# Two tiles' results in one bank, every second group's rows summed in three parts by VectorE, and the first taps ahead of the weights' loads, in a fused attention and feed-forward kernel

## The chip, the core and the metric

The kernel runs on one core of a Trainium2 chip. The metric is the time of one execution on the device, in microseconds (us). The engines of a core run at the same time and each takes its instructions in the order in which they stand: PE (TensorE) multiplies matrices, DVE (VectorE) and ACT (ScalarE) work element by element and reduce, POOL (GpSimd) works element by element on SBUF alone, and SP (SyncE) issues most of the transfers. An instruction that waits holds back all that stand behind it on its engine.

## What is computed

A local attention over windows of seven positions, and on its result a feed-forward block: a product with `w_in`, a SoLU (h times softmax of h), a layer norm and a product with `w_out`. Cut to what matters:

```python
w = softmax(weight_gen)                        # over the 7 taps, per position and head
out[s] = sum(w[s, k] * x_pad[s + k] for k in range(7))     # heads of 24 columns, 192 in all
x = out.reshape(33280, 192)
h = x @ w_in                                   # 192 -> 1024
solu = h * softmax(h)
ln = (solu - mean(solu)) / sqrt(var(solu) + 1e-6) * g_ln
return ln @ w_out                              # 1024 -> 192
```

There are 8 sequences of 4160 positions: 33280 rows, in 260 tiles of 128 rows.

## The kernel before

Each of the 128 partitions holds a run of 260 consecutive positions, so that a tile t is position t of every run. The work goes through five engines, tile by tile:

- **POOL** makes the attention for a group of four tiles at once (`attention`, called by `attend`; the first four tiles go in two groups of two). One product makes seven weighted rows `pr` (L174, 5376 elements a partition); an addition puts parts 3 to 5 on parts 0 to 2 (L180, 2304 elements); a second one makes two parts `half` of the four that are left (L182, 1536 elements). POOL also makes two of the seven steps of the taps' softmax (`softmax_taps`: the subtraction L114 and the scaling L126), once per chunk. A chunk is what is loaded at once: 4, then 8, then 8 tiles, then 16.
- **DVE** adds the two parts of `half` into the rows `a` (`last_sum`, L433, the step `fin`). `half` has two buffers, `a` has three.
- **PE** transposes `a` (step `xT`, two tiles at a time, L450), ACT and DVE split the result into a high and a low half, and PE multiplies with `w_in` in twelve matmuls (`first_product`, step `mm1`, L491 and L494) into a PSUM tile `h` of two banks, of which there are three.
- DVE finds the maximum (L505), ACT the exponentials (L509), DVE their product with h (L515), ACT the squares (L521) and the high half of the result (L528), DVE the low half (L532). `h` is free after these.
- SP transposes the result by a DMA (`transpose_s`, L540) into one of six buffers `hlT`; PE multiplies it with `w_out` in 24 matmuls (`second_product`, step `mm2`, L580) into `po`, one bank of PSUM with one buffer; ACT scales `po` into the output rows (`finish`, step `out`, L591), and SP stores four tiles at once.

At the start the weights, which come as pairs of 32-bit words, are converted by DVE and ACT (`float_of_double`, L241 to L260), and the first product waits for that. The squares of x (L145) and their sums (L151) feed a scale.

The order of all these steps on each engine is not written out: `issue_order` is a planner that holds a cost and the earlier steps for each step, and at each moment gives an engine the step with the lowest key among those that are ready. The key is the tile's number plus an offset per kind of step, from the table `URGENCY`. What comes out is the program's fixed order. The steps ahead of the planner (loads, constants, the first chunk's taps) stand in the order of the code.

Of the kernel before, what the change touches and what calls it, by code (L numbers as in the profile page):

```python
# [26 lines left out]
def tile_kernel(ctx: ExitStack, tc: tile.TileContext, x, weight_gen, w_in, w_out, g_ln, out):  # L27
    nc = tc.nc
# [24 lines left out]
    ps_a = ctx.enter_context(tc.tile_pool(name="ps_a", bufs=1, space=PSUM))  # L53
    ps_o = ctx.enter_context(tc.tile_pool(name="ps_o", bufs=1, space=PSUM))

    nc.scalar.preload_act_table_set("natural_log_exp_and_others")

    x_run = x.rearrange("b (q t) d -> (b q) t d", t=RUN)
# [112 lines left out]
    def attention(xt, wt, t, n, half):  # L171

        pr = att.tile([P, K, TG, D], F32, name="pr", bufs=1)[:, :, :n]
        nc.gpsimd.tensor_tensor(  # L174
            out=window(pr, 0, [(TG * D, K), (HG, n * H), (1, HG)]),
            in0=window(xt, t * D, [(D, K), (HG, n * H), (1, HG)]),
            in1=window(wt, t * HK, [(1, K), (K, n * H), (0, HG)]),
            op=ALU.mult,
        )
        nc.gpsimd.tensor_tensor(out=pr[:, :3], in0=pr[:, :3], in1=pr[:, 3:6], op=ALU.add)  # L180

        nc.gpsimd.tensor_tensor(  # L182
            out=half, in0=window(pr, 0, [(2 * TG * D, 2), (D, n), (1, D)]),
            in1=window(pr, TG * D, [(5 * TG * D, 2), (D, n), (1, D)]), op=ALU.add,
        )
# [2 lines left out]
    w_in = w_in.bitcast(I32)  # L188
    w_out = w_out.bitcast(I32)
    load_x(0)  # L190
    raw_a = att.tile([P, 2 * FF], I32, name="raw_a", bufs=1)

    raw_b = big.tile([P, FF], I32, name="hl", bufs=3)
# [29 lines left out]
    column = const.tile([P, 1], F32, name="column")  # L223
    minus = const.tile([P, P], F32R, name="minus")
    nc.vector.tensor_scalar_mul(minus, ident, -1.0)

    for step in range(TAP_STEPS):
        softmax_taps(0, step)

    scratch = {}  # L230

# [50 lines left out]
    def norm_of_first(step):  # L282
        if step < 3:
            nc.vector.tensor_reduce(
                sq[:, 4 + step : 5 + step], first["b" if step == 2 else step], axis=AX.X,
                op=ALU.max, apply_absolute_value=True,
            )
        elif step == 3:
            nc.scalar.activation(sq[:, 4:7], sq[:, 4:7], AF.Square)
        elif step == 4:  # L290
            first["total"] = ps_o.tile([P, 512], F32, name="po")
            nc.tensor.matmul(first["total"][:, :3], ones, sq[:, 4:7], start=True, stop=True)
        elif step == 5:
            nc.vector.tensor_reduce(
                first["total"][:, 8:9], first["total"][:, :3], axis=AX.X, op=ALU.add
            )
        elif step == 6:
            nc.scalar.activation(column, first["total"][:, 8:9], AF.Ln, scale=1.05 * FF)
            nc.scalar.activation(column, column, AF.Exp, scale=0.5)
# [27 lines left out]
    def scale_and_sum(f, step):  # L327
        if "w2" not in second:
            second["w2"] = att.tile([P, NJ, D], F32, name="raw_a", bufs=1)
        w2 = second["w2"]  # L330
        j0, j1 = JP * f, JP * (f + 1)
        if step == 0:
            for j in range(j0, j1):
                nc.scalar.activation(
                    w2[:, j, :], second[f][:, (j - j0) * D : (j - j0 + 1) * D], AF.Copy,
                    scale=g[:, j : j + 1],
                )
        elif step == 1:
            if f == 0:
                second["sums"] = ps_o.tile([P, 512], F32, name="po")  # L340
            for j in range(j0, j1):
                nc.tensor.matmul(
                    second["sums"][:, :D], ones, w2[:, j, :], start=j == 0, stop=j == NJ - 1
                )
        elif step == 2:
            junk = big.tile([P, FH], F32, name="frac")
            nc.scalar.activation(
                junk[:, : JP * D], w2[:, j0:j1].rearrange("p j d -> p (j d)"), AF.Square,
                accum_out=sq[:, f : f + 1],
            )  # L350
# [54 lines left out]

    def stat_group(t):

        n = 2 if t < 2 * TG else TG
        return n if t % n == n - 1 else 0


    def group(t):

        if t < TG:
            return 2 if t % 2 == 0 else 0
        return TG if t % TG == 0 else 0

    def attend(t):
        n = group(t)
        c = max(n for n in range(NCHUNK) if starts[n] <= t)  # L420
        half = att.tile([P, 2, TG, D], F32, name="half", bufs=2)[:, :, :n]
        half_of[t] = half
        attention(xs[c], ws[c], t - starts[c], n, half)

# [148 lines left out]
    def second_product(t):  # L573
        hlT = hlT_of.pop(t)

        free = t >= RUN - TG and t % 2 == 1
        po = ps_h.tile([P, FF], F32, name="h") if free else ps_o.tile([P, 512], F32, name="po")
        terms = [(half, j, w) for j in range(NJ) for half, w in ((0, 0), (0, 1), (1, 0))]
        for n, (half, j, w) in enumerate(terms):
            nc.tensor.matmul(  # L580
                po[:, :D], hlT[:, half * NJ + j, :], w2_hl[:, j, w, :],
                start=n == 0, stop=n == len(terms) - 1,
            )
        p_of[t] = po
# [58 lines left out]


URGENCY = dict(
    a00=3.1, a01=2.3, a02=-28.9, a03=-6.5, a04=-3.6, a10=80, a11=-25.4, a12=-13, a13=-10, a14=10.4,
    attA=85.1, attB=2.4, b0=120.9, b1=-144.6, b2=138.3, b3=-1.5, b4=54.3, c00=-28.1, c01=85.1,
    c02=6.8, c10=-25.3, c11=31.3, c12=-72.7, c20=99.4, c21=-5.6, c22=10.2, c30=-149.7, c31=-14.5,
    c32=-100.3, dup=52.6, exp=-129.5, f0=8.2, f1=-120.4, f2=-71.5, f3=-118.4, f4=-66.1, f5=-45.6,
    fin=18.4, hi=-11, lo=33, lw=18.7, lx0=10.2, lx1=-115.4, lx2=-109.1, lx3=-20.7, max=-30,  # L650
    mm1=25.5, mm2=0.4, n0=-7.5, n1=11.8, n2=-1.8, n3=-113.6, n4=-8.6, n5=-69, n6=-123.6, od=-6.9,
    out=-81.2, p30=22.9, p31=0.5, p4=9.7, p5=12.6, p6=11.6, p70=-10.2, p71=-8.7, p80=20.3, p81=5.9,
    q00=7.1, q01=-5.1, q02=118.9, q10=-15.7, q11=20.7, q12=16.8, q20=100.6, q21=-95.2, q22=20.4,
    q30=143.8, q31=81.5, q32=98.3, solu=-7.6, sq=5, t0=5.1, t1=-3.7, t2=77.9, t3=44.1, t4=-26.5,
    t5=110.1, t6=267.2, tr=-13, v00=170.9, v01=5.1, v02=44, v03=0.2, v1=54.2, v2=58.8, v3=-12.2,
    v4=1, v5=21.2, xT=-66.9, xhi=-46.7, xld=30,
)


def issue_order(run, starts, group, stat_group, loads):  # L660
# [5 lines left out]

    PE, DVE, ACT, SP, POOL = range(5)
    SAME, CROSS = (25, 127, 143, 0, 102), 130
    free = [3000, 5900, 5000, 12000, 9050]
    steps, number = [], {}  # L670

    def add(name, t, engine, cost, *after, ready=0):
# [7 lines left out]
    parts = ["a0", "b", "a1", *(f"c{f}" for f in range(4))]  # L680
    for n, part in enumerate(parts):
        w_in, size = n < 3, 512 if n < 3 else 384
        at = (9000, 10500, 12000)[n] if w_in else 15000
        before = () if w_in else (f"{parts[n - 3]}4", "n" + {"a0": "0", "a1": "1", "b": "2"}[parts[n - 3]]) if n < 6 else ("q00",)
        if n:
            before += (parts[n - 1] + "0",)
        once(part + "0", DVE, 3 * (60 + size), *before, ready=at)
        once(part + "1", ACT, 2 * (190 + 0.85 * size), part + "0")
        once(part + "2", DVE, 3 * (60 + 1.04 * size), part + "1")
        if w_in:  # L690
            once(part + "3", ACT, 190 + 0.75 * size, part + "2")
            once(part + "4", DVE, 60 + 1.04 * size, part + "3")
            once("n" + {"a0": "0", "a1": "1", "b": "2"}[part], DVE, 60 + 1.04 * size, part + "2")
        else:
            f = n - 3
            once(f"q{f}0", ACT, 700, part + "2")
            once(f"q{f}1", PE, 660, f"q{f}0", *([f"q{f - 1}1"] if f else ["n6"]))
            once(f"q{f}2", ACT, 520, f"q{f}0")
    add("p30", 0, DVE, 868, ("q31", 0), ("mm1", 1))
# [31 lines left out]
        add("v4", t, DVE, 80, ("v3", t))  # L731
        add("v5", t, ACT, 240, ("v4", t))

    add("v00", 0, ACT, 1800, ready=9000)
    add_norms(0, 0)
    for c in range(1, len(starts) - 1):
        t, before = starts[c], starts[c - 1] if c > 1 else -1
# [7 lines left out]
        for part in range(4 if whole else 1):  # L745
# [3 lines left out]
                load = min(part + 1, loads - 1) if whole else loads - 1  # L749
                add(f"v0{part}", t, ACT, size, (f"lx{load}", t))  # L750
            else:
                add(f"v0{part}", t, ACT, size, ready=15000)
        add_norms(c, t)
        n = (starts[c + 1] - t) * 8
        on = (DVE, POOL, ACT, DVE, ACT, DVE, POOL)
# [13 lines left out]
    for i, t in enumerate(groups):  # L769
# [3 lines left out]
            after.append(("t6", starts[c]))  # L773
        if c > 1:
            after.append((f"lx{loads - 1}", starts[c]))
        add("attA", t, POOL, 14990 if full else 7500, *after, ready=15000 if c == 1 else 9000)
        add("attB", t, POOL, 3510 if full else 1800, ("attA", t), ("fin", groups[i - 2] if i > 1 else -1))
        old = t // 4 * 4 - 12
        add("dup", t, ACT, 307 if full else 200, ("fin", t))
        add("fin", t, DVE, 1710 if full else 880, ("attB", t), ("xT", old + 2 if old >= 0 else -1))  # L780


    def on_vector(t):
# [15 lines left out]
    for t in range(run):  # L799
# [15 lines left out]
        if t >= run - 4:  # L815
            after += [("mm1", run - 1), ("out", t - 2)]
        else:
            after.append(("out", t - 1))
        add("mm2", t, PE, 2170, ("tr", t), *after)
        add("out", t, ACT, 304, ("mm2", t), ("f5", stats_of[t]), ("od", t // 4 * 4 - 5))  # L820
        if n := stat_group(t):
            tiles = range(t - n + 1, t + 1)
            add("f0", t, ACT, 190, ("v5", starts[chunk_of(t)]), *(("exp", u) for u in tiles))
# [101 lines left out]
```

## Time and profile before

| what | us |
|---|---|
| median of three runs | 1347.44 |
| lowest and highest run | 1345.54, 1348.4 |
| the profiled execution's own time | 1347.67 |
| its span, first to last instruction | 1345.8 |
| its mean granted TensorE clock | 0.994 |
| POOL's last instruction ends | 1290.43 |

A row of a time line has its start, its length, the engine, the line of the kernel, the operation, and the tile that it writes and those that it reads; in brackets stands how long the engine was idle before it, and what ended that. A row of a group of equal instructions has their count, their busy time in all and the mean in ns of one, then the idle time ahead of them. A row of windows has busy time (and count) for each engine in that stretch, then the granted clock, the DMA engines' share and GB/s. PEld is the loading of weights into TensorE, beside its matmuls.

### The profile page before, as it was taken

The numbers are of one execution on the slowest core, as the hardware profiler recorded it, in microseconds if no ns is written. First come the engines' busy times: TensorE is split into PE (matmuls) and PEld (weight loads), VectorE is DVE, ScalarE is ACT, GpSimd is POOL, SyncE is SP. The second block draws the span as 40 slices with busy tenths as digits, with TensorE's granted clock in tenths as the row PEclk, the third lists the DMA queues.
The fourth block names the chain that finished last, engine by engine and source line by source line (L and its number), as shares of the span: only waits on it lengthen the run. The fifth ranks groups of instructions, "written<-read, shape, count | busy, mean of one in ns | idle before, by whom it ended". The sixth has DMA issues, their size and how long they took to land.

```text
span 1345.8 us, 25810 instructions
## 1 busy us (share of the span) xinstructions
PE 1246.8 (93%) x9900; PEld 970.8 (72%) x9900; DVE 1210.2 (90%) x1588; ACT 1162.8 (86%) x2318; POOL 1247.7 (93%) x241
## 2 busy tenths in 40 slices
PE   0588899999999999999999999999999999999997
PEld 0365677777777777777777777777777777777776
DVE  5988899999999999999999999999999999889994
ACT  3778889889898988989898998989898898988886
POOL 5989899999999999999999999999999999999930
PEclk9899999999999999999999999999999999999999
DMA  5277668797886889688797968878787877976776
GB/s 180 74 159 169 139 134 201 123 207 137 155 179 134 196 137 208 125 179 163 129 202 140 191 140 180 162 128 203 140 193 137 183 150 138 183 134 123 133 134 130
DMA packets 565307, 210.31 MB, mean 156 GB/s; under 512 B 544456, under 2 KB 545864, under 8 KB 565184
## 3 DMA queue, kind: packets, MB, share of 16 engines
q1 hardware_dynamic: 563208, 206.55, 75.7%
q10 hardware_dynamic: 1976, 2.12, 0.6%
q8 instruction: 78, 1.28, 0.4%
q14 instruction: 45, 0.37, 0.1%
HBM read 46.15 MB, written 25.56 MB: 53 GB/s over the span
## 4 chain that ended last, share of the span: by engine, by line
ACT 43%; DVE 35%; issue 11%; PE 7%; DMA 2%; POOL 1%; SPq 0%; ACTq 0%; POOLq 0%
ACT hl L528 12%; ACT e L521 12%; DVE h L515 11%; DVE hl L532 11%; ACT e L509 9%; DVE stats L505 5%; DVE a L433 4%; ACT junk L145 3%; PE po L580 3%; PE h L494 2%; ACT x_hi L458 2%; ACT ot L591 2%; DMA hlT<-hl 2%; PE h L491 1%; DVE x_lo L479 1%
## 5 line engine op out<-in xcount | busy, mean ns | idle before, releaser
L174 POOL TENSOR_TENSOR pr<-xt,wt 128x5376 f32<-128x5376 f32 (+1 forms) x66 | 631.6, 9569 | 2.7
L580 PE MATMUL po<-w_hl,hlT 128*128 128x192 f16 x6192 | 555.1, 246 | 17.3 <-ACT ot L591 12.6
L580 PEld LDWEIGHTS <-hlT 128*128 128x128 f16 x6240 | 505.9, 98 | 83.2 <-issue 75.5
L515 DVE SCALAR_TENSOR_TENSOR h<-h,row,e 128x1024 f32<-128x1024 f32 x260 | 333.8, 1285 | 19.1 <-ACT e L509 16.9
L528 ACT ACTIVATE hl<-h 128x1024 f16<-128x1024 f32 x260 | 266.0, 1029 | 98.4 <-DVE h L515 55.4
L532 DVE SCALAR_TENSOR_TENSOR hl<-h,hl 128x1024 f16<-128x1024 f32 x260 | 316.5, 1218 | 36.8 <-ACT e L521 34.4
L180 POOL TENSOR_TENSOR pr<-pr 128x2304 f32<-128x2304 f32 (+1 forms) x66 | 333.0, 5045 | 5.2
L505 DVE TENSOR_REDUCE stats<-h 128x1 f32<-128x1024 f32 x260 | 316.3, 1217 | 3.9 <-PE h L494 3.3
L509 ACT ACTIVATE e<-h,stats 128x1024 f32<-128x1024 f32 x260 | 293.3, 1128 | 16.1 <-DVE stats L505 15.5
L521 ACT ACTIVATE e<-h,stats 128x1024 f32<-128x1024 f32 x260 | 293.0, 1127 | 1.1 <-DVE hl L532 1.0
L494 PE MATMUL h<-wa_hi,x_hi 128*128 128x512 f32 x520 | 234.0, 450 | 0.0
L182 POOL TENSOR_TENSOR half<-pr 128x1536 f32<-128x1536 f32 (+1 forms) x66 | 225.8, 3421 | 5.2
L494 PE MATMUL h<-wa_lo,x_hi 128*128 128x512 f32 x520 | 206.4, 397 | 0.0
L494 PE MATMUL h<-wa_hi,x_lo 128*128 128x512 f32 x520 | 205.9, 396 | 0.0
L494 PEld LDWEIGHTS h<-wa_hi,x_hi 128*128 128x128 f32 x520 | 98.1, 189 | 107.1 <-issue 95.5
L491 PE MATMUL h<-wb_hi,x_hi 64*128 64x512 f32 x520 | 131.0, 499 | 17.1 <-DVE hl L532 11.2
L433 DVE TENSOR_REDUCE a<-half 128x768 f32<-128x1536 f32 (+1 forms) x66 | 117.2, 1776 | 0.0
L591 ACT ACTIVATE ot<-po,stats 128x192 f32<-128x192 f32 x258 | 112.4, 436 | 3.6 <-PE po L580 3.6
L494 PEld LDWEIGHTS h<-wa_hi,x_lo 128*128 128x128 f32 x520 | 98.4, 189 | 23.2
L494 PEld LDWEIGHTS h<-wa_lo,x_hi 128*128 128x128 f32 x520 | 99.0, 190 | 12.0
L491 PE MATMUL h<-wb_hi,x_lo 64*128 64x512 f32 x520 | 104.2, 395 | 0.0
L450 PE MATMUL pa<-ident,a 128*128 128x128 f32 x520 | 81.2, 278 | 23.9 <-DVE x_lo L479 13.2
(89 smaller groups left out, 1072.0 us busy)
## 6 DMA issues: line engine op xcount, KB each, us to landing
out_dram<-ot SPq DMA_DIRECT2D x65, 384.0 KB, 3.3
xt<-in_x_dram SPq DMA_DIRECT2D x30, 576.0 KB, 4.8
xt<-in_x_dram SPq DMA_DIRECT2D x30, 480.0 KB, 4.4
wt<-in_weight_gen_dram SPq DMA_DIRECT2D x15, 448.0 KB, 4.8
hlT<-hl SPq DMA_TRANSPOSE x260, 4.7
xt<-in_x_dram SPq DMA_DIRECT2D x3, 384.0 KB, 4.6
raw_a<-in_moe_w_in_dram ACTq DMA_DIRECT2D x2, 512.0 KB, 7.4
raw<-in_moe_w_out_dram ACTq DMA_DIRECT2D x1, 768.0 KB, 12.2
```

The costliest lines, as they stand in the source:

```text
L174: nc.gpsimd.tensor_tensor(out=window(pr, 0, [(TG * D, K), (HG, n * H), (1, HG)]), in0=window(xt, t * D, [(D, K), (HG, n * H), (1, HG)]), i ...
L180: nc.gpsimd.tensor_tensor(out=pr[:, :3], in0=pr[:, :3], in1=pr[:, 3:6], op=ALU.add)
L182: nc.gpsimd.tensor_tensor(out=half, in0=window(pr, 0, [(2 * TG * D, 2), (D, n), (1, D)]), in1=window(pr, TG * D, [(5 * TG * D, 2), (D, n), ...
L491: nc.tensor.matmul(h[:, fs], lhs[rows, 1, :], rhs[rows], start=n == 0, stop=False)
L494: nc.tensor.matmul(h[:, fs], lhs[:, 0, :], rhs[:, fs], start=False, stop=n == 2)
L505: nc.vector.tensor_reduce(stat(t, NMAX), h_of[t], axis=AX.X, op=ALU.max, negate=True)
L509: nc.scalar.activation(e, h_of[t], AF.Exp, bias=stat(t, NMAX), accum_out=stat(t, Z))
L515: nc.vector.scalar_tensor_tensor(out=h, in0=h, scalar=row(t, SCALE), in1=e, op0=ALU.mult, op1=ALU.mult, accum_out=stat(t, M))
L521: nc.scalar.activation(e_of.pop(t), h_of[t], AF.Square, bias=stat(t, M), scale=-float(FF), accum_out=stat(t, Q),)
L528: nc.scalar.activation(hl[:, 0, :], h_of[t], AF.Copy, scale=2.0**14)
L532: nc.vector.scalar_tensor_tensor(out=hl[:, 1, :], in0=h_of[t], scalar=2.0**14, in1=hl[:, 0, :], op0=ALU.mult, op1=ALU.subtract,)
L580: nc.tensor.matmul(po[:, :D], hlT[:, half * NJ + j, :], w2_hl[:, j, w, :], start=n == 0, stop=n == len(terms) - 1,)
```

## The change

- One PSUM tile `results` of one bank is made at the start. A second product writes columns 0 to 191 of its first or second half, by the tile's number odd or even; in the planner a second product now follows the evacuation of the tile two before, not of the one before. The small sums of the preparation use the same bank.
- In every second group of four tiles (t // 4 odd, 32 of them) POOL leaves three parts: the addition over 2304 elements writes to `half` directly, and one over 768 elements puts the seventh part on the first. DVE's sum reads three parts there. `half` has room for three parts in both buffers.
- The last four tiles go in two groups of two, for the attention and for the statistics.
- The first chunk's taps are put ahead of the loads of the weights in the code.
- The planner has a new table `URGENCY` and new costs and ready times.

```diff
+    results = ps_o.tile([P, 512], F32, name="po")
...
+        if half.shape[1] == 3:
+            nc.gpsimd.tensor_tensor(out=half, in0=pr[:, :3], in1=pr[:, 3:6], op=ALU.add)
+            nc.gpsimd.tensor_tensor(out=half[:, 0], in0=half[:, 0], in1=pr[:, 6], op=ALU.add)
+            return
         nc.gpsimd.tensor_tensor(out=pr[:, :3], in0=pr[:, :3], in1=pr[:, 3:6], op=ALU.add)
...
     load_x(0)
+    for step in range(TAP_STEPS):
+        softmax_taps(0, step)
     raw_a = att.tile([P, 2 * FF], I32, name="raw_a", bufs=1)
...
-    for step in range(TAP_STEPS):
-        softmax_taps(0, step)
...
-            first["total"] = ps_o.tile([P, 512], F32, name="po")
+            first["total"] = results[:, 384:]
...
-                second["sums"] = ps_o.tile([P, 512], F32, name="po")
+                second["sums"] = results
...
-        n = 2 if t < 2 * TG else TG
+        n = 2 if t < 2 * TG or t >= RUN - TG else TG
...
-        if t < TG:
+        if t < TG or t >= RUN - TG:
...
+    def parts(t):
+
+        return 3 if t // TG % 2 else 2
...
-        half = att.tile([P, 2, TG, D], F32, name="half", bufs=2)[:, :, :n]
+        half = att.tile([P, 3, TG, D], F32, name="half", bufs=2)[:, : parts(t), :n]
...
-        po = ps_h.tile([P, FF], F32, name="h") if free else ps_o.tile([P, 512], F32, name="po")
+        po = ps_h.tile([P, FF], F32, name="h") if free else results[:, t % 2 * 256 :]
...
-    a00=3.1, a01=2.3, a02=-28.9, a03=-6.5, a04=-3.6, a10=80, a11=-25.4, a12=-13, a13=-10, a14=10.4,
+    a00=0.7, a01=13.5, a02=111.2, a03=-14.2, a04=63.6, a10=-30.7, a11=-18.7, a12=20.5, a13=-10.6,
...
-    free = [3000, 5900, 5000, 12000, 9050]
+    free = [3000, 5600, 7700, 12000, 6200]
...
-            after.append(("out", t - 1))
+            after.append(("out", t - 2))
...
-        add("out", t, ACT, 304, ("mm2", t), ("f5", stats_of[t]), ("od", t // 4 * 4 - 5))
+        add("out", t, ACT, 304, ("mm2", t), ("out", t - 1), ("f5", stats_of[t]), ("od", t // 4 * 4 - 5))
```

On POOL, in the first 60 us after its first full group, the order before is this, from the scaling of the third chunk's taps (`wt<-wt,wy`) on; `wt<-wt,wm` is the subtraction for a later chunk:

```order
L126 TENSOR_TENSOR wt<-wt,wy 128x448
L114 TENSOR_TENSOR wt<-wt,wm 128x896
L174 TENSOR_TENSOR pr<-xt,wt 128x5376
L180 TENSOR_TENSOR pr<-pr 128x2304
L182 TENSOR_TENSOR half<-pr 128x1536
L126 TENSOR_TENSOR wt<-wt,wy 128x896
L174 TENSOR_TENSOR pr<-xt,wt 128x5376
```

At the same place of the changed kernel:

```order
L128 TENSOR_TENSOR wt<-wt,wy 128x448
L176 TENSOR_TENSOR pr<-xt,wt 128x5376
L183 TENSOR_TENSOR half<-pr 128x2304
L184 TENSOR_TENSOR half<-half,pr 128x768
L116 TENSOR_TENSOR wt<-wt,wm 128x896
L176 TENSOR_TENSOR pr<-xt,wt 128x5376
```

The subtraction for the next chunk moved from ahead of the group's product to behind the group, and the group (tiles 12 to 15) ends in three parts.

On ACT, at the start of the program, the order before is this (`wt` are the taps, `raw_a`, `raw_101` and `g` the weights, `junk,squares_x` the squares of x):

```order
L79 DMA xt<-in_x_dram 15x1152 x4
L195 DMA raw_a<-in_moe_w_in_dram 128x1024 x2
L202 DMA raw_101<-in_moe_w_out_dram 128x4x384
L206 DMA g<-in_moe_g_ln_dram 128x8x1
L118 ACTIVATE wt<-wt 128x224
L145 ACTIVATE junk,squares_x<-xt 128x1920
L122 ACTIVATE wy<-wm 128x32
```

and in the changed kernel:

```order
L81 DMA xt<-in_x_dram 15x1152 x4
L203 DMA raw_a<-in_moe_w_in_dram 128x1024
L120 ACTIVATE wt<-wt 128x224
L203 DMA raw_a<-in_moe_w_in_dram 128x1024
L124 ACTIVATE wy<-wm 128x32
L210 DMA raw_111<-in_moe_w_out_dram 128x4x384
L214 DMA g<-in_moe_g_ln_dram 128x8x1
L147 ACTIVATE junk,squares_x<-xt 128x1920
```

The taps' exponentials moved ahead of three of the four loads of weights that ACT issues, and the copy of their sum (`wy<-wm`) ahead of two of them.

On DVE, at the same place, before (`h<-raw_a` and `h<-hl` convert weights, `wm<-wt` are the taps' maximum and sum):

```order
L112 TENSOR_REDUCE wm<-wt 128x32
L225 TENSOR_SCALAR minus<-ident 128x128
L241 TENSOR_SCALAR h<-raw_a 128x512
L244 TENSOR_SCALAR h<-raw_a 128x512
L246 TENSOR_SCALAR h<-h 128x512
L241 TENSOR_SCALAR h<-hl 128x512
L244 TENSOR_SCALAR h<-hl 128x512
L120 TENSOR_REDUCE wm<-wt 128x32
L246 TENSOR_SCALAR h<-h 128x512
L124 RECIPROCAL wy<-wy 128x32
```

and in the changed kernel:

```order
L114 TENSOR_REDUCE wm<-wt 128x32
L233 TENSOR_SCALAR minus<-ident 128x128
L122 TENSOR_REDUCE wm<-wt 128x32
L126 RECIPROCAL wy<-wy 128x32
L153 TENSOR_REDUCE row<-squares_x 128x1
L246 TENSOR_SCALAR h<-raw_a 128x512
```

The taps' sum and reciprocal moved from among the conversions to ahead of them, and so did the sum of the squares of x.

More of the change, by code (lines that the diff above doesn't have):

```diff
@@ L645 @@
 URGENCY = dict(
-    a00=3.1, a01=2.3, a02=-28.9, a03=-6.5, a04=-3.6, a10=80, a11=-25.4, a12=-13, a13=-10, a14=10.4,
[L647 to L656, printed above, removed]
+    a00=0.7, a01=13.5, a02=111.2, a03=-14.2, a04=63.6, a10=-30.7, a11=-18.7, a12=20.5, a13=-10.6,
+    a14=14.4, attA=-132.8, attB=16.3, b0=-141.9, b1=2.8, b2=-0, b3=-122.3, b4=14.7, c00=8,
+    c01=-82.5, c02=12.3, c10=-65.3, c11=3.9, c12=-10.1, c20=11.3, c21=-6.1, c22=-65.9, c30=3.4,
+    c31=128.1, c32=58.3, dup=3.4, exp=-66.2, f0=-7.4, f1=-6.5, f2=-37, f3=-129.8, f4=13.2,
+    f5=-62.7, fin=40.2, hi=-129.6, lo=6.2, lw=3.4, lx0=114.9, lx1=10.9, lx2=88.8, lx3=9.5, max=0.2,
+    mm1=140.7, mm2=147.9, n0=-0.3, n1=38.3, n2=-142.7, n3=-6, n4=-58.8, n5=-37.2, n6=-82.8,
+    od=-24.6, out=-60.7, p30=50.9, p31=-7.2, p4=19.3, p5=-40.3, p6=34.8, p70=10.4, p71=21.2,
+    p80=29.2, p81=39.2, q00=13.2, q01=1.2, q02=-93.1, q10=33.2, q11=108.1, q12=116, q20=-17.4,
+    q21=-54.3, q22=10.8, q30=13.2, q31=8.8, q32=72.3, solu=-32, sq=21.5, t0=161.8, t1=30.9, t2=3.9,
+    t3=49.1, t4=135.5, t5=133.4, t6=-88.8, tr=105.7, v00=67.1, v01=134.5, v02=-1.4, v03=9, v1=5.6,
+    v2=147.4, v3=2.9, v4=8.5, v5=-2.5, xT=-25.5, xhi=-6.6, xld=10.8,
 )
@@ L682, in issue_order @@
         w_in, size = n < 3, 512 if n < 3 else 384
-        at = (9000, 10500, 12000)[n] if w_in else 15000
+        at = (12000, 12000, 12500)[n] if w_in else 20000
         before = () if w_in else (f"{parts[n - 3]}4", "n" + {"a0": "0", "a1": "1", "b": "2"}[parts[n - 3]]) if n < 6 else ("q00",)
@@ L695, in issue_order @@
             f = n - 3
-            once(f"q{f}0", ACT, 700, part + "2")
+            once(f"q{f}0", ACT, 700, part + "2", "a02", "a12")
             once(f"q{f}1", PE, 660, f"q{f}0", *([f"q{f - 1}1"] if f else ["n6"]))
@@ L732, in add_norms @@
         add("v5", t, ACT, 240, ("v4", t))
-    add("v00", 0, ACT, 1800, ready=9000)
+    add("v00", 0, ACT, 1800, ready=10000)
     add_norms(0, 0)
@@ L751, in issue_order @@
             else:
-                add(f"v0{part}", t, ACT, size, ready=15000)
+                add(f"v0{part}", t, ACT, size, ready=21500)
         add_norms(c, t)
@@ L775, in issue_order @@
             after.append((f"lx{loads - 1}", starts[c]))
-        add("attA", t, POOL, 14990 if full else 7500, *after, ready=15000 if c == 1 else 9000)
-        add("attB", t, POOL, 3510 if full else 1800, ("attA", t), ("fin", groups[i - 2] if i > 1 else -1))
+        three = t // 4 % 2
+        add("attA", t, POOL, (9790 if three else 14990) // (1 if full else 2), *after, ready=21500 if c == 1 else 10000)
+        add("attB", t, POOL, (6950 if three else 3510) // (1 if full else 2), ("attA", t), ("fin", groups[i - 2] if i > 1 else -1))
         old = t // 4 * 4 - 12
         add("dup", t, ACT, 307 if full else 200, ("fin", t))
-        add("fin", t, DVE, 1710 if full else 880, ("attB", t), ("xT", old + 2 if old >= 0 else -1))
+        add("fin", t, DVE, (2500 if three else 1710) // (1 if full else 2), ("attB", t), ("xT", old + 2 if old >= 0 else -1))
     def on_vector(t):
```

## The prediction

> **What bounds the kernel now.** I read the page first (busy shares and tenths), then the time line of POOL in the body, then the windows, then the time line of PE where POOL no longer leads.
>
> ```profile
> span 1345.8 us, 25810 instructions
> PE 1246.8 (93%) x9900; PEld 970.8 (72%) x9900; DVE 1210.2 (90%) x1588; ACT 1162.8 (86%) x2318; POOL 1247.7 (93%) x241
> POOL 5989899999999999999999999999999999999930
> ```
> Four engines lie between 86% and 93%, so the averages name no bound. The tenths do: POOL is full from the second slice and stops 55 us before the end.
>
> ```profile
> 170.64 1.75 POOL L126 TENSOR_TENSOR wt<-wt,wy 128x896 f32<-128x896 f32 x1
> 172.35 9.70 POOL L174 TENSOR_TENSOR pr<-xt,wt 128x5376 f32<-128x5376 f32 x1
> ...
> 1216.38 9.71 POOL L174 TENSOR_TENSOR pr<-xt,wt 128x5376 f32<-128x5376 f32 x1
> 1226.18 5.12 POOL L180 TENSOR_TENSOR pr<-pr 128x2304 f32<-128x2304 f32 x1
> 1231.37 3.46 POOL L182 TENSOR_TENSOR half<-pr 128x1536 f32<-128x1536 f32 x1
> 1234.91 9.71 POOL L174 TENSOR_TENSOR pr<-xt,wt 128x5376 f32<-128x5376 f32 x1
> ```
> A group of four tiles takes POOL 1234.91 - 1216.38 = 18.53 us from start to start, without a wait. A chunk of 16 tiles is four of these and two passes over the taps of 1.71 us (172.35 - 170.64): 77.5 us, **4.85 us a tile**. The tiles do go by at that pace, as PE's first products show (the first row of tiles 0, 28, 239 and 259; tiles counted by the rows of L505):
>
> ```profile
> 45.84 0.79 PE L491 MATMUL h<-wb_hi,x_hi 64*128 64x512 f32 x2
> ...
> 202.60 0.50 PE L491 MATMUL h<-wb_hi,x_hi 64*128 64x512 f32 x2
> ...
> 1228.47 0.50 PE L491 MATMUL h<-wb_hi,x_hi 64*128 64x512 f32 x2
> 1233.49 0.50 PE L491 MATMUL h<-wb_hi,x_hi 64*128 64x512 f32 x2
> 1237.97 0.50 PE L491 MATMUL h<-wb_hi,x_hi 64*128 64x512 f32 x2
> 1242.45 0.50 PE L491 MATMUL h<-wb_hi,x_hi 64*128 64x512 f32 x2
> 1247.35 0.50 PE L491 MATMUL h<-wb_hi,x_hi 64*128 64x512 f32 x2
> 1252.50 0.50 PE L491 MATMUL h<-wb_hi,x_hi 64*128 64x512 f32 x2
> ...
> 1323.30 0.51 PE L491 MATMUL h<-wb_hi,x_hi 64*128 64x512 f32 x2
> ```
> Tiles 28 to 239 took (1228.47 - 202.60) / 211 = 4.862 us each: **POOL bounds the body**. Near the end PE has a backlog and runs without a wait: tiles 240 to 244 took 1252.50 - 1233.49 = 19.01 us, two pairs of transposes among them, so PE's floor is **4.753 us a tile**, only 2.2% under POOL's pace. What the other engines need in the body:
>
> ```profile
> core 0: us, PE busy (x) PEld busy (x) DVE busy (x) ACT busy (x) POOL busy (x), PEclk, DMA share, GB/s
> 200.00:1200.00 1000.00, 974.80 (x7809) 759.34 (x7807) 925.88 (x1193) 897.45 (x1784) 985.75 (x181) 1.00 0.81 163
> 45.84:200.00 154.16, 129.05 (x935) 97.32 (x935) 134.98 (x183) 128.14 (x263) 142.50 (x30) 0.94 0.64 133
> ```
> 1000 us are 205.7 tiles, so DVE works 4.50 us a tile and ACT 4.36.
>
> **The change, part by part.** *Every second group in three parts.* The rows that price it, of whole and of half groups:
>
> ```profile
> L182 POOL TENSOR_TENSOR half<-pr 128x1536 f32<-128x1536 f32 x64 | 222.2, 3471 | 5.0
> L182 POOL TENSOR_TENSOR half<-pr 128x768 f32<-128x768 f32 x2 | 3.6, 1814 | 0.2
> L433 DVE TENSOR_REDUCE a<-half 128x768 f32<-128x1536 f32 x64 | 115.3, 1801 | 0.0
> L433 DVE TENSOR_REDUCE a<-half 128x384 f32<-128x768 f32 x2 | 1.9, 954 | 0.0
> ```
> In such a group the addition over 2304 elements stays, and that over 1536 (3.47 us) becomes one over 768 (1.81): 1.66 us less, 53 us over 32 groups. A group then takes 16.87 us, a chunk 2 x 18.53 + 2 x 16.87 + 3.43 = 74.2 us, 4.64 us a tile: POOL falls below PE's floor. VectorE's sum over three parts reads 2304 elements for 1536. No row has that size; by the two forms 768 elements more cost 1801 - 954 = 847 ns, so 2.65 us; from below it can't be shorter than the 1.80 it was, from above I take 1801 x 1.5 = 2.70. Twice a chunk that is 0.106 us a tile: DVE needs 4.50 + 0.11 = 4.61.
>
> So PE (4.753) and DVE (4.61) become the bound together. The floor of the pace is 4.753. Its upper end I take from the fullest stretch that DVE shows:
>
> ```profile
> 600.00:650.00 50.00, 48.60 (x394) 38.02 (x391) 47.64 (x62) 46.35 (x94) 49.19 (x10) 1.00 0.80 164
> DVE stats L552 <- ACT e L521: 31.9, 39, 1.1
> DVE hl L532 <- ACT e L521: 24.5, 40, 2.1
> DVE h L515 <- ACT e L509: 12.2, 24, 0.8
> PE po L580 <- ACT ot L591: 4.1, 11, 0.4
> ```
> (The last four are the waits of DVE and PE between 200 and 1200 us.) 47.64 of 50 us is 95.3%; at that share 4.61 us of work take 4.84. DVE's waits are all short ones on ACT, and ACT has 8% left at PE's floor, so I take the middle, **4.79**. Tiles 28 to 259 then take 231 x 4.79 = 1106.5 us for 1323.30 - 202.60 = 1120.7: **14.2 us less** (22.8 at the floor, 2.7 at 4.84).
>
> *Two results in one bank.* A second product no longer waits for the evacuation of the tile before, but of the one before that. In the body that wait is 4.1 us of 1000 and hidden by POOL's bound; where PE is the bound it would be 0.02 us a tile, 4.7 us in all. It is inside the 4.79; nothing queues for it. The row shows waits on one buffer, and cannot show what two engines in one bank do. The Trainium skill (PSUM — Partial Sum Buffer, PSUM bank collisions raise a hardware error) asks that TensorE and an evacuating engine be kept apart by bank, not by address, and says that the chip reports an error and does not stall; no run here shows it. Kept apart as it asks, the wait would stay and the sum would be some 4.7 us higher; without, it is as it stands.
>
> *The new order.* ACT, DVE and PE are reordered throughout (up to three second products in a row on PE); no instruction but those above is added in the body, so it is priced through the pace. On SP the loads of taps move ahead of those of rows; the transposes keep their order, and a product now follows its tile by up to seven places for five, which six buffers allow.
>
> *The start.* Rows of POOL, ACT and DVE:
>
> ```profile
> 8.86 0.39 ACT L118 ACTIVATE wt<-wt 128x224 f32<-128x224 f32 x1 [6.84 <-issue]
> 10.85 0.19 ACT L145 ACTIVATION_READ_ACCUMULATOR junk<-xt 128x1 f32 x1
> 12.38 0.69 DVE L241 TENSOR_SCALAR h<-raw_a 128x512 int32<-128x512 int32 x1 [9.09 <-DMA raw_a<-in_moe_w_in_dram]
> 17.08 0.58 POOL L126 TENSOR_TENSOR wt<-wt,wy 128x224 f32<-128x224 f32 x1 [13.26 <-DVE wy L124]
> 38.12 0.97 POOL L126 TENSOR_TENSOR wt<-wt,wy 128x448 f32<-128x448 f32 x1 [0.42 <-DVE wy L124]
> 81.17 1.75 POOL L114 TENSOR_TENSOR wt<-wt,wm 128x896 f32<-128x896 f32 x1 [3.37 <-DVE wm L112]
> 150.48 1.76 POOL L114 TENSOR_TENSOR wt<-wt,wm 128x896 f32<-128x896 f32 x1 [6.33 <-DVE row L151]
> ```
> The exponentials of the first taps stand behind ACT's issues of the weights' loads; now three loads stand behind them, and the taps' sum and reciprocal ahead of the conversion that DVE starts at 12.38. POOL's first product can start near 9 us for 17.7. Of these 8.7 us some 4 remain, since the next chunk's reciprocal (38.12) still stands behind the conversion of the weights. ACT's loads of the second half of the weights and of the second matrix go later by about 1 us (two ACT rows of 0.39 and 0.23, and two hops); DVE reaches their data long after they land, and if that cover went, it would cost that 1 us. DVE's conversion also stands behind a sum over ACT's squares now, which ended at 11.0 and end near 12: it may slip by up to 1 us. The stalls of 3.37 and 6.33 us go too, since those steps now stand behind the group's products. PE's first product (45.84) hangs on DVE's conversions and stays within 1 us.
>
> Tiles 0 to 28 took 202.60 - 45.84 = 156.8 us; PE's floor is 28 x 4.753 = 133.1, so at most 23.7 us are to be had, at least none. DVE worked 134.98 of the 154.16 us up to 200; with three longer sums (2.5) at the 96% of the body that is 143: **11 us less**, which I take.
>
> *The end.* The last four tiles go in two groups of two, in sums and in statistics. The last transposes ran well ahead of their products (PE's backlog above), so POOL's earlier end is not late there; 1345.8 - 1323.30 = 22.5 us stay.
>
> **Sum.** 1345.8 - 14.2 - 11 = 1320.6 us of span; the profiled execution took 1347.67 us, 1.87 more than its span, so 1322.5. It lies 0.2 over the median (1347.44): **1322 us**.
>
> **The rivals.**
> - *The forecast*, 1310 to 1333: 0.64.
> - *PE runs at its floor throughout*: start and body at their full 23.7 and 22.8: 1301. For it: PE's unbroken stretch. Against: DVE at 97%, above any window. 0.09.
> - *DVE caps the body* at 95.3%: 4.84, 2.7 us there, and perhaps 6 at the start: 1339. For it: no window is fuller. Against: those windows had POOL as bound. 0.17.
> - *Slower*: DVE, with a fixed order and sums of 2.65 us standing ahead of what frees the three buffers of h, waits as much as now. Its idle share is 7.4% (74.1 of 1000): 4.61 / 0.926 = 4.98 us a tile, 231 x 4.98 = 1150, 30 more; less 11 it gives 1366. It decides from 4.90 us a tile (94% busy), where the start's gain is eaten. For it: second products come in twos and threes, so h arrives in bursts. Against: the idle time now is made by POOL's pace. 0.09.
> - *PE is no floor*: its matmul rows overlap. DVE would bound at 100%: 191.6 + 231 x 4.61 + 22.5 + 1.9 = 1281. Starts 19.01 us apart for four tiles without a listed wait, at clock 1.00, speak against it: 0.01. The Trainium skill (Perfetto Trace Analysis, Identifying the Most-Contended Engine) judges TensorE's headroom by the share of weight loads, not by matmul time; that is 72% here, a quarter free, and by it this rival would be the forecast; the rows of starts do not bear it out.
>
> **The numbers.** Under 0.2% (2.7 us) a measurement of this kernel tells nothing from no change. Faster: 0.64 + 0.09 + 0.01 and 0.15 of the DVE cap, 0.89; same: 0.02 of the cap and 0.01 of the slower case, 0.03; slower 0.08. The range reaches from near PE's floor (1304) to past the cap (1342); the slower case and the last rival are left out, and the ends of the others.
>
> **What would show it.** POOL: rows of 768 elements (1.8 us) in 32 groups, its share below 97% in the body, waits on DVE where it has none. DVE: 32 sums near 2.65 us and 95 to 97% busy. PE: 4.77 to 4.82 us a tile between tiles 28 and 239, no wait on the evacuation. Start: POOL's first product near 9 us, PE's first near 46, tile 28 near 191. It is wrong if DVE stays at 93% busy at a pace over 4.84, if PE waits on ACT or DVE in the body for more than 15 us, or if tile 28 comes no earlier than now.

## The result, and the profile after

The changed kernel takes 1379.07 us (median of four runs, 1375.32 to 1381.75) beside 1347.88 of the kernel before: 1.0233 times as long, 95% interval 1.0206 to 1.026. It was predicted at 1322, faster. The profiled execution took 1381.75 us.

The page of the changed kernel: span, busy shares, POOL's tenths, and the chain of work that ended last (followed back from the last instruction, at each step to what released it) by engine.

```profile
span 1379.9 us, 25912 instructions
PE 1257.9 (91%) x9900; PEld 983.1 (71%) x9900; DVE 1240.0 (90%) x1592; ACT 1166.3 (85%) x2323; POOL 1195.8 (87%) x244
POOL 7999998998999989998999899898999899999100
PE 39%; DVE 21%; ACT 14%; issue 6%; DMA 4%; SPq 1%; ACTq 0%; DVEq 0%
```

The chain of the kernel before, a part of its page that the prediction did not read:

```profile
ACT 43%; DVE 35%; issue 11%; PE 7%; DMA 2%; POOL 1%; SPq 0%; ACTq 0%; POOLq 0%
```

POOL works 52 us less than before (1195.8 for 1247.7), DVE 30 us more (1240.0 for 1210.2), PE 11 us more. POOL had held 1% of the chain before, although its tenths were full; ACT and DVE held 78%. After, PE leads with 39%.

A window of the body (200 to 1200 us, columns as in the prediction), and PE's first products of tiles 28, 239 and 259:

```profile
200.00:1200.00 1000.00, 943.01 (x7446) 737.26 (x7445) 916.78 (x1152) 868.91 (x1727) 936.13 (x179) 0.99 0.77 157
```
```profile
191.99 0.50 PE L500 MATMUL h<-wb_hi,x_hi 64*128 64x512 f32 x2
...
1261.83 0.50 PE L500 MATMUL h<-wb_hi,x_hi 64*128 64x512 f32 x2
...
1355.54 0.50 PE L500 MATMUL h<-wb_hi,x_hi 64*128 64x512 f32 x2
```

All five engines lost share in the body, DVE too in spite of its longer sums (916.78 for 925.88), so there are new waits. Tiles 28 to 239 took (1261.83 - 191.99) / 211 = 5.07 us each, for 4.86 before. Tile 28 is 10.6 us earlier than its 202.60 before, near the 11 that were predicted. From there to tile 259 the changed kernel takes 1163.6 us for 1120.7, so the body gave back the 10.6 us and 32 more. Waits of the changed kernel over the whole span, in us, times and longest:

```profile
ACT ot L600 <- PE po L589: 66.2, 64, 2.3
...
POOL wt L128 <- DVE wy L126: 49.5, 14, 6.4
...
PE po L589 <- ACT ot L600: 18.7, 26, 2.6
```

and two of these rows before, for the same tiles under their old lines:

```profile
PE po L580 <- ACT ot L591: 12.6, 16, 2.7
...
ACT ot L591 <- PE po L580: 3.6, 4, 1.6
```

An evacuation is the step `out`, in which ACT copies a second product's result out of PSUM. ACT waits 66 us for second products ahead of its evacuations, for 4 us before. This is the new wait. What it waits for is seen in the time lines of PE and of ACT around one of them:

```profile
855.96 0.63 PE L503 MATMUL h<-wa_hi,x_lo 128*128 128x512 f32 x1
856.39 5.07 PE L589 MATMUL po<-w_hl,hlT 128*128 128x192 f16 x48
861.39 0.50 PE L500 MATMUL h<-wb_hi,x_hi 64*128 64x512 f32 x2
```
```profile
857.33 0.88 ACT L147 ACTIVATE junk<-xt 128x768 f32<-128x768 f32 x1
858.07 0.22 ACT L147 ACTIVATION_READ_ACCUMULATOR junk<-xt 128x1 f32 x1
858.16 1.04 ACT L537 ACTIVATE hl<-h 128x1024 f16<-128x1024 f32 x1
861.50 0.42 ACT L600 ACTIVATE ot<-po,stats 128x192 f32<-128x192 f32 x1 [2.29 <-PE po L589]
861.82 1.11 ACT L518 ACTIVATE e<-h,stats 128x1024 f32<-128x1024 f32 x1
```

A second product has 24 matmuls, so the 48 are two of them, one for each half of the bank. In a window that ends with the first of the two, its row stands alone:

```profile
856.39 3.09 PE L589 MATMUL po<-w_hl,hlT 128*128 128x192 f16 x24
```

The first one is done at 856.39 + 3.09 = 859.48. ACT is ready at 859.20 and still does not evacuate it then; it starts at 861.50, when the second one has ended (856.39 + 5.07 = 861.46). The compiled program says why: `results` is one tile, and waits are set for the tile, not for its halves. An evacuation that is recorded (put into the program's order) behind the next tile's product waits for that product too. In the changed order this is so for 80 of the 260 evacuations; before, for none. In the trace all 80 start after the next tile's product has ended. The idle time ahead of them is 63.4 us, and only 0.3 us of it lies before the end of their own products. Behind the waiting evacuation stand the exponentials of the next tile (L518), and DVE's next row comes after an idle 2.94 us:

```profile
863.40 0.17 DVE L561 TENSOR_REDUCE stats<-stats 128x4 f32<-128x12 f32 x1 [2.94 <-ACT stats L570]
```

### The profile page after: what moved, and what is told of

It reads as the page before. It is cut to its first block, busy times and chain, and to the rows that moved or that the text cites. A ratio compares the mean times of both kernels' runs of the same rounds, so it can differ in the third digit from the quotient of the medians.

```text
span 1379.9 us, 25912 instructions
## 1 busy us (share of the span) xinstructions
PE 1257.9 (91%) x9900; PEld 983.1 (71%) x9900; DVE 1240.0 (90%) x1592; ACT 1166.3 (85%) x2323; POOL 1195.8 (87%) x244
## 4 chain that ended last, share of the span: by engine, by line
PE 39%; DVE 21%; ACT 14%; issue 6%; DMA 4%; SPq 1%; ACTq 0%; DVEq 0%
PE po L589 19%; PE h L503 11%; PE h L500 6%; DVE h L524 6%; DVE hl L541 5%; DVE stats L514 5%; ACT e L530 4%; ACT hl L537 3%; ACT e L518 3%; DVE a L442 2%; DMA xt<-in_x_dram 2%; PE pa L459 2%; DVE x_lo L488 2%; DMA hlT<-hl 1%; ACT ot L600 1%
## 5 line engine op out<-in xcount | busy, mean ns | idle before, releaser
L589 PE MATMUL po<-w_hl,hlT 128*128 128x192 f16 x6192 | 550.5, 247 | 19.0 <-ACT ot L600 18.7
L589 PEld LDWEIGHTS <-hlT 128*128 128x128 f16 x6240 | 515.6, 98 | 60.8 <-issue 57.0
L518 ACT ACTIVATE e<-h,stats 128x1024 f32<-128x1024 f32 x260 | 290.9, 1120 | 13.5 <-DVE stats L514 11.5
L186 POOL TENSOR_TENSOR pr<-pr 128x2304 f32<-128x2304 f32 (+1 forms) x35 | 169.1, 4830 | 2.7
L500 PE MATMUL h<-wb_hi,x_hi 64*128 64x512 f32 x520 | 131.2, 500 | 42.7 <-DVE hl L541 18.7
L183 POOL TENSOR_TENSOR half<-pr 128x2304 f32<-128x2304 f32 x32 | 163.9, 5121 | 2.5
L600 ACT ACTIVATE ot<-po,stats 128x192 f32<-128x192 f32 x258 | 108.9, 423 | 67.4 <-PE po L589 66.2
L442 DVE TENSOR_REDUCE a<-half 128x768 f32<-128x2304 f32 (+1 forms) x67 | 149.3, 2229 | 0.0
L500 PEld LDWEIGHTS h<-wb_hi,x_hi 64*128 64x128 f32 x520 | 49.6, 185 | 98.6 <-issue 35.5
L188 POOL TENSOR_TENSOR half<-pr 128x1536 f32<-128x1536 f32 (+1 forms) x35 | 115.1, 3290 | 2.7
```

The costliest lines, as they stand in the source:

```text
L442: nc.vector.tensor_reduce(columns(t)[:, :, :D], half.rearrange("p j t d -> p t d j"), axis=AX.X, op=ALU.add)
L500: nc.tensor.matmul(h[:, fs], lhs[rows, 1, :], rhs[rows], start=n == 0, stop=False)
L518: nc.scalar.activation(e, h_of[t], AF.Exp, bias=stat(t, NMAX), accum_out=stat(t, Z))
L589: nc.tensor.matmul(po[:, :D], hlT[:, half * NJ + j, :], w2_hl[:, j, w, :], start=n == 0, stop=n == len(terms) - 1,)
```

## The experiments

Fifteen variants were run; the table below brings the main ones together. All ratios are to the kernel before, run beside them. Its medians there were 1347.1 to 1349.0 us, so the difference of two variants is good to about 2 us.

**The parts of the change in the old order.** Three parts alone, the bank alone, the taps alone, and the three together, each with the order of before:

```diff
 # e1_parts: before, and
+        if half.shape[1] == 3:
+            nc.gpsimd.tensor_tensor(out=half, in0=pr[:, :3], in1=pr[:, 3:6], op=ALU.add)
...
 # e2_bank: before, and
+    results = ps_o.tile([P, 512], F32, name="po")
...
 # e3_taps: before, and
+    for step in range(TAP_STEPS):
+        softmax_taps(0, step)
     raw_a = att.tile([P, 2 * FF], I32, name="raw_a", bufs=1)
...
 # e4_all_old_order: before, with all three
```

> The kernel before, its fixed order untouched, with the three parts alone (32 groups). Theory O (the new order costs the time, the parts as such do not): POOL's 53 us go, the body falls from 4.862 us a tile towards PE's floor of 4.753, time 1322 to 1340. Rival P (DVE's 32 sums of 2.65 us are what the engines wait for): as slow as the changed kernel in the body, 5.0 us a tile, 1375 or more.

> The kernel before, its fixed order untouched, with the two results in one bank alone. Theory O: POOL still bounds at 4.862 us a tile, 1343 to 1348. Rival B (a matmul and an evacuation in one bank slow each other): rows of the second product's matmuls over 246 ns or of the evacuation over 436 ns, and 1355 or more.

> The kernel before, with the first chunk's taps ahead of the weights' loads and nothing else (two parts everywhere, one bank for one result, the order before). Theory POOL: POOL's first product starts near 9 us for 17.7 and the gain stays: 1336 to 1341 us. Theory chain: POOL's earlier start is worth little, 1343 to 1348.

> The kernel before with its planner's order, and in it all three edits: three parts, two results in one bank, first taps ahead of the weights' loads. Theory O: 1312 to 1335, POOL no longer full, PE the bound. Rivals P and B: 1370 or more, as the changed kernel.

Measured: three parts 1373.55 us, 1.0192 [1.0177, 1.0207]; bank 1349.93, 1.0013 [1.0004, 1.0023]; taps 1344.44, 0.9979 [0.9968, 0.9989]; all three 1370.24, 1.0168 [1.0146, 1.019]. So the three parts, which were to bring the gain, cost 25 us by themselves in the old order. One bank for two results costs 2 us or less where evacuations stand ahead of the next product; a matmul of the second product took 247 ns for 246. The taps first bring 3.5 us; POOL's first product starts at 13.92 for 17.73, not near 9, since in the old order DVE's reciprocal still stands behind a conversion of weights, which starts at 12.24 when its load has landed. Where POOL's saved time went, with three parts alone, is in its waits (the body's window, then POOL's one long wait there):

```profile
200.00:1200.00 1000.00, 954.77 (x7642) 743.14 (x7642) 933.36 (x1169) 880.83 (x1750) 926.05 (x177) 1.00 0.79 160
```
```profile
POOL wt L126 <- DVE stats L559: 63.9, 12, 5.9
```

**Each half of the three parts alone.** In e8 POOL leaves three parts and DVE sums two of them, so POOL has 53 us less and DVE's sums are as before (the third part is left out of the result). e7 and e10 lengthen DVE's part alone.

```diff
 # e8_pool_shorter: e1_parts, and
-        half = half_of.pop(t)
+        half = half_of.pop(t)[:, :2]
 # e7_dve_longer: before, with a third part of zeros in constant tiles, and
+        if t // TG % 2:
+            half = full_of[t]
 # e10_dve_again: before, and behind DVE's sum
+        if t // TG % 2:
+            nc.vector.tensor_reduce(
+                columns(t)[:, :2, :D], half[:, :, :2].rearrange("p j t d -> p t d j"), axis=AX.X, op=ALU.add
+            )
```

> The kernel before in its own order, POOL making three parts in 32 groups (53 us less) and DVE summing two of them, as long as before; the third part is left out. Theory L: no gain, 1343 to 1349, POOL's time turns into waits for DVE. Rival, POOL alone bounds: 1318 to 1335.

> The kernel before in its own order, POOL's work as it was, and DVE's sum reading a third part of zeros in 32 groups (27 us more of DVE). Theory L (in the fixed order the chain through DVE and ACT is as full as POOL, so what DVE gets is paid in full): 1370 to 1378. Rival, POOL alone bounds and DVE's 7% idle are slack, as the prediction had it: 1346 to 1353.

> The kernel before, with one thing added: in every second group of four tiles VectorE repeats the first half of its sum over the two parts of half (768 elements, same result; the row of that size took 954 ns), so 32 x 0.95 = 30.5 us more of VectorE and nothing else; POOL is as before. This is VectorE's longer part of the change without POOL's shorter one. Theory POOL (the prediction's: POOL bounds the body, VectorE has 74 us idle in 1000): 1346 to 1354 us. Theory chain (VectorE and ScalarE pass the tiles to each other in a fixed order and are as full as POOL; VectorE's idle time is hand-offs): about 25 us more, 1366 to 1378, as the three parts alone showed (1373.6).

Measured: e8 1348.77 us, 0.9995 [0.9986, 1.0005]; e7 1390.92, 1.0309 [1.0289, 1.033]; e10 1371.98, 1.0181 [1.0168, 1.0195]. e7 is flawed: its constant tiles let POOL's next group be recorded ahead of DVE's sum, which then waited for it, 17 us once at the start (and the sums are of other rows). Its time says nothing on this, though its body goes at 4.97 us a tile, for 4.96 in e1 and in e10. e8 and e10 have no such flaw. The windows of e8 and of e10, then the repeated sum of e10:

```profile
200.00:1200.00 1000.00, 974.03 (x7797) 758.37 (x7795) 925.24 (x1191) 896.84 (x1784) 945.32 (x180) 1.00 0.81 163
```
```profile
200.00:1200.00 1000.00, 954.77 (x7643) 743.13 (x7641) 933.20 (x1194) 881.00 (x1748) 966.98 (x178) 1.00 0.78 160
```
```profile
L437 DVE TENSOR_REDUCE a<-half 128x384 f32<-128x768 f32 x32 | 31.3, 977 | 1.1
```

In e8 POOL's share falls from 98.6% to 94.5% and the time does not move: 53 us of POOL are worth nothing. In e10 POOL is as it was and 31 us of DVE, which had idled 74 us in 1000, cost 24 us. So POOL does not set the pace of the old order alone. What DVE has to do sets it, with ACT in the same chain, as the chain of work said; POOL, full as it was, kept the same pace. At 4.85 of 4.86 us a tile POOL would be the next bound at once, and no run shortens ACT or DVE alone in this order.

**The changed order, with and without the wait.** e5 is the changed kernel with two parts everywhere; e9 with three parts of which DVE sums two (the third left out). In e6, e14 and e15 the 80 late evacuations read a constant in SBUF (these tiles' results are left out), so neither waits for the other; otherwise e6 is the changed kernel, e14 has two parts, e15 DVE's short sums (third part left out).

```diff
 # e5, e14
-        return 3 if t // TG % 2 else 2
+        return 2
 # e9, e15
-        half = half_of.pop(t)
+        half = half_of.pop(t)[:, :2]
 # e6, e14, e15
+    late = {t for t in range(RUN - TG) if place["mm2", t + 1] < place["out", t]}
...
+        if t in late:
+            po = wa_hi.bitcast(F32)
         nc.scalar.activation(ot[:, t % TG, :], po[:, :D], AF.Copy, scale=stat(t, OUT))
```

> The changed kernel in its new order, with two parts in every group (POOL has its 53 us again, DVE loses its 27). Theory O: still slow, 1365 to 1400, since the same rows stand in the same places. Rival P: DVE is relieved and POOL bounds at 4.85 us a tile from tile 28 at 192, 1340 or so.

> The changed kernel in its new order; in the tiles whose evacuation is recorded behind the next tile's second product (some 80 of 260) the evacuation reads a constant of SBUF for the product's result, so these tiles' results are left out and their evacuations wait for no product. Theory W (in one tile of PSUM such an evacuation waits for the next product as well, and holds ACT): the 66 us of ACT's waits for second products fall under 15, the body from 5.04 us a tile to 4.80 to 4.87, time 1325 to 1345. Rival O (the new order is slow with or without this wait): 1368 or more.

> The changed kernel in its new order, with DVE summing two of the three parts (27 us less of DVE; the third part is left out). Theory W: ACT's waits on the second products stay, 1358 to 1380. Rival, DVE's longer sums make the loss: 1345 to 1352.

> The changed kernel's order without the wait, as in the run at 1345.7 us (the same tiles' results left out), with two parts in every group: POOL gets 53 us back, VectorE loses 27. If POOL bounds once the wait is gone (the planner of the change was right to want three parts), this is slower than 1345.7: 1352 to 1375. If POOL bounds nothing there, VectorE's shorter sums show: 1330 to 1345.

> The same order without the wait, POOL in three parts, of which VectorE sums two (the third is left out), so VectorE's sums are as short as before and POOL 53 us shorter: all the reliefs of the change and none of its costs. If VectorE's longer sums are what the order without the wait still pays for: 1322 to 1336. If they lie beside other work there: 1340 to 1346.

Measured: e5 1380.19, 1.0241 [1.022, 1.0262]; e6 1345.74, 0.9974 [0.9963, 0.9986]; e9 1371.32, 1.0165 [1.0145, 1.0186]; e14 1366.34, 1.0146 [1.0129, 1.0163]; e15 1336.87, 0.9922 [0.9905, 0.9939]. Medians in us:

| order, evacuations | two parts | three parts, DVE sums two | three parts |
|---|---|---|---|
| before | 1347.9 | 1348.8 (e8) | 1373.6 (e1) |
| changed, with the wait | 1380.2 (e5) | 1371.3 (e9) | 1379.1 (after) |
| changed, without it | 1366.3 (e14) | 1336.9 (e15) | 1345.7 (e6) |

With the three parts, the wait costs 1379.1 - 1345.7 = 33 us. (e6 came out just above the 1325 to 1345 that were expected, and its body at 4.92 us a tile, not 4.80 to 4.87: the wait is not all of the loss.) The evacuations that read SBUF are not shorter (460 ns for 426 of the others), so it is the wait that went, and with it PE's wait the other way (L589 for ACT, 18.7 us, now 8.7). In the changed order without the wait POOL is a bound: two parts are 20.6 us slower than three. The chain of e14 says so by itself, and DVE waits for `half` (the granted clock was 0.984 in e14 and 0.990 in e6; what that adds was not separated):

```profile
POOL 51%; PE 16%; DVE 12%; ACT 9%; issue 7%; DMA 4%; SPq 1%; POOLq 0%; ACTq 0%; DVEq 0%
```
```profile
L442 DVE TENSOR_REDUCE a<-half 128x768 f32<-128x1536 f32 x63 | 113.3, 1799 | 25.3 <-POOL half L188 25.2
```

DVE's longer sums cost 1345.7 - 1336.9 = 9 us there, not 25. With the wait in place DVE's sums cost much the same (1379.1 - 1371.3 = 8 us), but POOL's relief falls from 29 us (1366.3 - 1336.9) to 9 (1380.2 - 1371.3).

**Can the three parts pay without the wait?** In e11 the planner puts a second product behind the evacuation of the tile before, and the table is a new one, found for that rule; e12 does the same with three parts in every fourth group (and one cost of the planner changed). e13 is e1 with the evacuations of tiles 4 to 255 reading a constant (their results left out).

```diff
 # e11, e12: after, with another table, and
-            after.append(("out", t - 2))
+            after.append(("out", t - 1))
 # e12
-        return 3 if t // TG % 2 else 2
+        return 3 if t // TG % 4 == 3 else 2
 # e13: e1_parts, and
+        if TG <= t < RUN - TG:
+            po = wa_hi.bitcast(F32)
```

> The changed kernel with all its parts (three parts in every second group, one bank, taps first), but its planner holds a second product behind the evacuation of the tile before, as the one bank does on the chip, and URGENCY is a new table found for that rule; so no evacuation stands behind the next tile's product. Theory: the 33 us are the wait alone, and the rest of the change can gain if the order around the three parts is a good one: 1332 to 1346 us, with ScalarE's waits on the second product below 5 us. Rival: three parts in every second group cost VectorE their 25 us in any order: 1362 to 1374.

> As the run with the wait in the planner, with three parts in every fourth group only and a table found for that: POOL gets 27 us less than before, VectorE 14 us more. Theory: 1332 to 1344 us, near the run before or a little under it. Rival (VectorE's longer sums are paid in any order): half of 25 us over the kernel before with taps first, 1354 to 1360.

> The kernel before with the three parts alone (1373.6 us so far), in which ScalarE's evacuations of tiles 4 to 255 read a constant of SBUF and not the result of the second product; these tiles' results are left out. So second products and evacuations no longer wait for each other, in the old order. Theory order (the old order itself holds VectorE's longer sums on its path; evacuations have no part in it, PE waits on them for 1.8 us of 1000): 1366 to 1375. Theory link (any coupling of product and evacuation makes the longer sums cost, and without it they are free as in the run without the wait): 1343 to 1352.

Measured: e11 1371.44, 1.0159 [1.014, 1.0178]; e12 1356.37, 1.005 [1.0034, 1.0065]; e13 1373.9, 1.0198 [1.0183, 1.0214]. My theory for e11 and e12 fell: the new table did bring ACT's waits for the product down, but not the time. Both times lie in the ranges of the rival, by which DVE's longer sums are paid in full in any order; e6 and e15 speak against it, since there these sums cost 9 us. What holds e11 was not separated. e13 shows that in the old order the evacuations have no part in the 25 us. The waits of e11 on both sides of an evacuation:

```profile
PE po L589 <- ACT ot L600: 29.9, 15, 4.5
...
ACT ot L600 <- PE po L589: 9.2, 10, 3.2
```

Here PE is held instead, up to 4.5 us at a time. The granted clock of e11's profile was also the lowest of all, 0.981 for 0.994 before; how much of its 22 us is that was not separated. No version that uses three parts and leaves nothing out was faster than the kernel before. Of all that leave nothing out, only the kernel before with the taps first is below both kernels: 1344.44 us, 0.2% under the kernel before.

## Why the prediction was wrong

- **"POOL bounds the body": wrong, the first step that failed.** The pace of POOL (4.85 us a tile) and of the tiles (4.862) agreed, and I took that for the cause. e8 takes 53 us from POOL and the pace stays (4.87, from the first products of tiles 28 to 239). What spoke against it was on the page: POOL held 1% of the chain. In e14, where POOL does bind, it holds 51%.
- **"The idle time now is made by POOL's pace": wrong, the same step seen from DVE.** It was the reason to let DVE rise to 95% and to give the slower rival 0.09. e10 adds 31 us to DVE alone and pays 24. DVE's 7% idle, hand-offs with ACT in a fixed order, took up only 7 us of the 31.
- **"A second product no longer waits ...; nothing queues for it": wrong, and the larger loss.** The order let products go ahead of the evacuation, but the bank's one tile made the evacuation wait for them: 33 us (e6). Queued behind it on ACT were the exponentials, and behind these DVE. I had priced the wait that was removed (4.7 us; 4.6 by its own row) and not the one it became. The Trainium skill (PSUM — Partial Sum Buffer, PSUM bank collisions raise a hardware error) asks for PE and the evacuating engine to be kept apart by bank, not by address; the program did keep them apart so (in the trace of the changed kernel no evacuation of the bank overlaps a matmul into it), and the price was not the 4.7 us that the prediction gave it. No run has both in one bank at a time, so what the chip would do then is not shown.
- **The pace of 4.79: not reached by any run.** Without the wait it is (1229.34 - 190.70) / 211 = 4.92 (e6, first products of tiles 28 and 239); with DVE's short sums as well, 4.89 (e15), still above the 4.86 of before. What holds e15 there was not separated; its chain is PE 48%, DVE 14%, ACT 13%, POOL 12%.
- **DVE's sum: mis-sized.** It was put at 2.65 us, at most 2.70; it took 2.81, 32 x 1.01 = 32 us in all for the 27 in the sum:

```profile
L442 DVE TENSOR_REDUCE a<-half 128x768 f32<-128x2304 f32 x32 | 89.9, 2811 | 0.0
L184 POOL TENSOR_TENSOR half<-half,pr 128x768 f32<-128x768 f32 x32 | 58.5, 1827 | 2.5
```

- **POOL's parts: right** (1.83 us for 1.81).
- **The start: right in its sum, in part by luck.** POOL's first product starts at 9.00 us, as predicted, and tile 28's first product at 191.99 (191 was predicted). But the 11 us were to come between tiles 0 and 28, with DVE 96% busy, and PE's first product was to stay within 1 us of 45.84. It came at 43.19, 2.7 us earlier, and tiles 0 to 28 took 148.8 us for 156.8, 8 us less, with DVE 92% busy (136.46 of 148.80 us). It needs the changed order: in the old one the taps bring 3.5 us.

```profile
8.34 0.58 POOL L128 TENSOR_TENSOR wt<-wt,wy 128x224 f32<-128x224 f32 x1 [4.41 <-DVE wy L126]
9.00 4.94 POOL L176 TENSOR_TENSOR pr<-xt,wt 128x2688 f32<-128x2688 f32 x1
```

- **The end: 2 us off.** From tile 259's first product (1355.54) to the end are 24.4 us, for the 22.5 kept.
- **The slower rival** had 1366 with chance 0.09 and named DVE's fixed order. It was the right side and, by e10, a right mechanism for part of the loss; it did not see the wait, and came 13 us short.

As a sum, from the first products of the profiled executions: the start brought 10.6 us, the end cost 2, and tiles 28 to 259 cost 42.9 (1163.6 for 1120.7), which makes the span 34 us longer. Without the wait (e6) these tiles take 1131.3 us, so 32 of the 42.9 are the wait. Of the other 10.6, DVE's longer sums make 7 (e15 takes 1124.4). The last 3.7 stay in spite of POOL's relief, and their cause is open.

## What to carry to other kernels

An engine that is full at the kernel's pace need not set it: look at its share of the chain, and take work from it alone before other engines are given more. Idle time of an engine that hands tiles to and fro with another in a fixed order is no room for work until a run with more work on that engine alone has shown it. Where two results share a tile, ask for each order of recording which of the two users waits for the other, and what stands behind the one that waits.

## What the runs showed of the hardware

VectorE's sum over parts took 954 ns for 384 results of two parts, 1801 for 768 results of two, and 2811 for 768 results of three. From the first to the second, 768 more elements cost 847 ns; from the second to the third, as many cost 1010. A price by elements alone came out 0.16 us too low for the third part; why is not shown.
